# One normalization for two groups of heads, an output projection over full rows, and another rule for starting exponentials on VectorE

## The chip, the cores and the metric

The kernel runs on one core of one Trainium2 chip. Its time is the device time of one launch in microseconds (us), the median of several runs. The profile is of one further execution. Its span runs from the first to the last instruction that the profiler saw; the device time of the same execution lies a little above the span.

## The reference

One adaLN transformer block over 2048 tokens of width 512, in bf16:

```python
mod = silu(c) @ w_mod                       # six vectors sa, ca, ga, sb, cb, gb of 512
h = layernorm(x) * (1 + ca) + sa
q, k, v = h @ wqkv                          # 32 heads of 16
p = softmax(q @ k.T * 16 ** -0.5)           # per head 2048 x 2048
x = x + ga * ((p @ v) @ wo)
h = layernorm(x) * (1 + cb) + sb
x = x + gb * ((gelu(h @ w_gate) * (h @ w_up)) @ w_down)      # inner width 1792
```

The 32 score matrices have 134 million entries, and each needs an exponential. That is 2048 tiles of 128 keys by 512 columns of queries.

## The kernel before, in words

**Attention.** The heads are taken in eight groups of four, numbered qd from 0 to 7. Group qd uses the 128-row chunk qd // 2 of the transposed q and k. A chunk holds eight heads of 16 rows, that is four strips of 32 rows with an even and an odd head each. An even qd takes the even heads (k in `kme`, with the odd heads' rows set to zero) and an odd qd the odd heads (`kmo`). The tokens, as queries, are cut into six sets (`SETS`): three of 512, one of 256, two of 128. A *unit* is one group of heads with one set of queries. For the first QS groups the two sets of 128 are joined to one unit of 256. So the last units in order are: before, the joined groups 0 to 4, then set 4 with groups 5, 6, 7, then set 5 with groups 5, 6, 7.

A unit runs through its keys in *rounds*; a round is four score tiles (banks of PSUM, 128 x 512), one for each head. The score matmuls (`qk`) of up to four banks run in four row strips of TensorE. Each bank then needs an exponential, and there are two ways:

- ScalarE takes two or three banks in one ACTIVATE (`E<-ps_sc`, 128x1024 or 128x1536) and writes to E, a ring of NSL slots.
- VectorE takes a whole round, a *quad*. One instruction for each bank turns the score into the bits of a bf16 number (`dreg<-ps_sc`, `mreg<-ps_sc`, or `<-ps_mi` where the bank of side work is borrowed). Then three *shifts* over 128x2048 (`mreg<-dreg`, `mreg<-mreg`), on VectorE or GpSimd, add constants to these bits, and the four results go through four passes of the value matmul, in place of one. Only rounds whose key tiles lie from QA to QB can be quads.

The value matmuls (`pv_mms`, `ps_pv<-E,vaug`) have 17 output rows for each head: 16 sums, and in row 16 the sum of the exponentials. The four heads of a unit stand in rows 0, 32, 64, 96 of the accumulator.

**End of a unit** (`unit_end`). VectorE copies the accumulator to `osb`. On the queue of SyncE (SP), a chain of DMAs brings the four rows of sums to DRAM and back over 128 partitions (`scr_den<-osb`, `den<-scr_den`), VectorE takes reciprocals (`rden<-den`), and DMAs write them to DRAM and spread each over 32 rows (`scr_rec<-rden`, four times `rb<-scr_rec`). VectorE multiplies (`onorm<-osb,rb`). A unit's range of `osb` is in `self.live` until then, and the last value matmul of a later unit that needs this range is held back (`blocked`). Groups 6 and 7 of the two last sets avoid the DMAs: `near_end` spreads the sums with a small matmul.

**Output projection.** `onorm` has eight slots, one for each group. Of its 128 rows only 4 x 16 are of use. `wo` has its rows placed to match, and zeros elsewhere. For each tile of 128 tokens `wo_mm` runs eight matmuls of 128 rows by 512 columns, and `mm` cuts each into four of 32 output rows (not in the tail).

**Order.** All instructions are written out ahead of time by one program. It keeps its own estimate of when each engine is free, and at each step (`stream`) appends either the next score matmuls with their exponentials, a value matmul, a piece of side work (projections, output projection, FFN, all through the one bank `ps_mi`), or a filler matmul that keeps TensorE busy. The position `pos` counts score banks from 0 to 2048. Each piece of side work has a first position and a due position, and `credit` grows so that it gets done in time. A quad begins only if a buffer and a candidate round are there and, past `ends[2]` (position 1536), only if the credit is below CREDIT, so while there is little side work owing. Element-wise steps and DMAs are tasks that are appended to VectorE, ScalarE or SP when the estimate says that they can start.

On the chip each engine works through its list in order, and waits where a semaphore is not there yet. SP's queue carries the chains of the sums, the weights of the FFN (256 KB each, streamed for the first four sets, then kept for the two last sets) and the outputs.

**The tail** (`tail`) comes after the last exponential: the FFN of the last two tiles, and for the last tile also the output projection and the second layernorm.

Of the kernel before, what the change touches and what calls it, by code (L numbers as in the profile page):

```python
# [32 lines left out]
BCOL = (0, 0, 0, 0, 0, 128)  # L33
QS = 5
CH = 3
SC = 2 * CH
NSL = 18
assert NSL % CH == 0
# [3 lines left out]
NS = 4  # L42
AHEAD = 20
PREFER = 300
LAND = 1500
SIDE = 1024
PRESS = 5
HOT = 1
# [5 lines left out]
SLIP = 0  # L54
QA = 5
QB = 13
# [402 lines left out]
class _Kernel(_Recorder):  # L459
# [12 lines left out]
    def alloc(self):  # L472
# [33 lines left out]
        self.kq = [mreg[:, 12288:14336], dreg[:, 0:2048], dreg[:, 2048:4096]]  # L506
        self.wo = sb("wo", [P, 8, D], BF16)
        self.E = sb("E", [P, NSL, 512], BF16)
        self.onorm = sb("onorm", [P, 8, 512], BF16)
        self.ga = sb("ga", [P, D], BF16)  # L510
# [313 lines left out]
    def side_mod(self):  # L824
        mi = self.mi[:, :]
        if not self.dry:
            self.task([lambda dc=dc: self.ts("dve", self.scbc[:, dc, :], self.ones, self.sc_bf[:, dc:dc + 1],
                                             None, ALU.mult) for dc in range(NDC)], "scbc")
        yield from self.until("scbc")
        for dst, k, s in ((self.ga, 2, 1.0), (self.gb, 5, 0.5)):  # L830
            for dc in range(NDC):
                yield 512, lambda dc=dc, k=k: self.mm(mi, self.scbc[:, dc, :], self.mod_w(dc, 512 * k, 512),
                                                      start=(dc == 0), stop=(dc == NDC - 1))
            self.ts("dve", dst[:, :], mi, s, None, ALU.mult)
            yield END
        if not self.dry:
            self.task([lambda qd=qd: self.tt("dve", self.wo[:, qd, :], self.wo[:, qd, :], self.ga[:, :], ALU.mult)
                       for qd in range(8)], "wo")
        yield 512, lambda: self.mod_cols(mi[:, 0:8], 1536)
        self.copy("dve", self.modB[:, :], mi[:, 0:8])  # L840
        self.ts("dve", self.modB[:, 4:8], self.modB[:, 4:8], 1.0, None, ALU.add)
        self.done("modB")
        if not self.dry:
            self.sq_free.extend(range(NS))
        yield END

    def side_wo_load(self):

        if not self.dry:
            self.task([lambda qd=qd: self.memset("dve", self.wo[:, qd, :], 0.0) for qd in range(8)]  # L850
                      + [lambda: self.memset("dve", self.self32[:, :], 0.0)], "wo0")
        yield from self.until("wo0")
        selv = self.self32[:, :].rearrange("p (a b) -> p a b", b=32)
        self.affine_select(selv, [[-32, 4], [0, 32]], ALU.not_equal, 1.0, -16, 1)
        for j in range(4):
            for ee in range(2):
                src = self.A_wo.rearrange("(a j e r) n -> j e r a n", j=4, e=2, r=DH)[j, ee]
                self.dma("sp", self.wo[32 * j:32 * j + DH, ee:8:2, :], src, "wo%d" % (2 * j + ee))
        yield END
# [24 lines left out]

    def wo_mm(self, bank, gi, tl, qd, first=True):
        c = OCOL[gi] + P * tl
        self.mm(bank, self.onorm[:, qd, c:c + P], self.wo[:, qd, :], start=first and qd == 0, stop=(qd == 7))

# [14 lines left out]
    def near_end(self, k, qd, den):  # L903

        q0, W = SETS[k]
        yield from self.until(("osb", k, qd))
        _, lo, hi = self.osb_span(((k,), qd, q0, W))
        osb, rb = self.osb[:, lo:hi], self.rb[:, lo:hi]
        yield 4 * W, lambda: self.mm(den, self.self32[:, :], osb)

        def fin():
            self.tt("dve", self.onorm[:, qd, OCOL[k]:OCOL[k] + W], osb, rb, ALU.mult)
        if not self.dry:
            self.task([lambda: self.recip(rb, den)], ("rec", k, qd))
        yield from self.until(("rec", k, qd))
        if not self.dry:
            self.task([fin], ("onorm", k, qd))
        yield END

    def side_wo(self, gi):  # L920
# [4 lines left out]
        yield from self.until("wo")  # L925
        for qd in range(8):
            yield from self.until(("onorm", gi, qd))
        for i in range(n):
            for qd in range(8):
                yield 512, lambda i=i, qd=qd: self.wo_mm(mi, gi, i, qd)  # L930
            self.wo_fin(mi, tiles[i])
# [281 lines left out]
    def stream(self):  # L1213
# [133 lines left out]
        while cg <= group[units[-1]]:  # L1347
# [12 lines left out]
            if tq is not None and tq <= t + 30:  # L1360
# [6 lines left out]
                if short > FILL - FLOOR or slack > 213 and short > 0:  # L1367
                    self.mm(self.scp[:, s0, :], *filler)
                    continue
                g = None  # L1370
                if len(mem) == CH and pos >= FIRST and not self.pressed() and self.free["dve"] + 600 < max(self.free["act"], t + 480) + 880 + LATE:
                    while quad is None and cand and rounds[cand[0]][2] < pos + (AHEAD1 if rounds[cand[0]][2] < nsplit else AHEAD):
                        cand.pop(0)
                    if quad is not None:
                        g = quad["rnd"][2]
                    elif (cand and self.quad_free and (pos < ends[2] or self.credit < CREDIT) and rounds[cand[0]][2] < pos + 96 and self.backlog() < BACK
                          and all(k in self.have for k in self.keys(seq[rounds[cand[0]][2]]))):
# [8 lines left out]
                if g is not None:  # L1386
                    for n in (CH, CH - 1):
                        if n == CH and (self.open or self.credit > SIDE
                                        or self.probe(lambda: self.mm(self.mi[:, 0:P], *filler)) > t + 30):
# [140 lines left out]
    def unit_end(self, u, acc):  # L1530
# [5 lines left out]
        if sets[0] >= len(SETS) - 2 and len(sets) == 1 and qd >= 6:  # L1536
            self.done(("osb", sets[0], qd))
            return
        self.live[u] = (lo, hi)
        m = 4 * W // P  # L1540
        o = 8 if BCOL[sets[0]] else 0
# [5 lines left out]
        def rd(j):  # L1547
            self.dma("sp", self.rb[32 * j:32 * j + 32, lo:hi],
                     s2[W * j:W * j + W].rearrange("(o n) -> o n", o=1).broadcast_to([32, W]), "dd%d%d" % (sem, j))

        def fin2():
            c = OCOL[sets[0]]
            self.tt("dve", self.onorm[:, qd, c:c + W], osb, rb, ALU.mult)
            if self.probing is None:
                self.live.pop(u)
                for k in sets:
                    self.done(("onorm", k, qd))

        def free():
            c = OCOL[sets[0]]  # L1560
            return ("den", u) in self.have and all(
                ("wo", k) in self.have for k in range(sets[0]) if OCOL[k] < c + W and c < OCOL[k] + SETS[k][1])
# [3 lines left out]
                  + [("sp", lambda j=j: rd(j)) for j in range(4)], ("den", u))  # L1566
        self.task([fin2], None, free)

# [46 lines left out]
    def tail_end(self, k):  # L1615
# [7 lines left out]
        yield lambda: self.mm(bank, self.ident[:, :], self.xs[:, tile, :], start=True, stop=False)  # L1623
        for qd in range(8):
            yield from self.until(("onorm", k, qd))
            yield lambda qd=qd: self.wo_mm(bank, k, 0, qd, False)
        self.task([lambda: self.ln_stat(tile, bank)] + self.ln2_steps(k, bank), ("ln2", k))
# [94 lines left out]
```

## Time and profile before

| | before |
|---|---|
| median of 7 runs | 824.65 us (823.65 to 829.19) |
| profiled execution: time | 825.47 us |
| profiled execution: span | 823.6 us |
| busy: TensorE, VectorE, ScalarE, GpSimd | 765.7, 682.4, 788.2, 225.8 us |
| E<-ps_sc 128x1024 and 128x1536 on ScalarE | 416 and 273 |
| scores to bf16 bits on VectorE | 396 (99 quads) |
| granted TensorE clock, mean | 0.996 |

The busy time of an engine is the time in which it had at least one instruction under way. ScalarE's instructions overlap a little: one starts before the last has ended, so the mean duration in a row of the profile is longer than the distance from start to start.

### The profile page before, as it was taken

The numbers are of one execution on the slowest core, as the hardware profiler recorded it, in microseconds if no ns is written. First come the engines' busy times: TensorE is split into PE (matmuls) and PEld (weight loads), VectorE is DVE, ScalarE is ACT, GpSimd is POOL, SyncE is SP. The second block draws the span as 40 slices with busy tenths as digits, with TensorE's granted clock in tenths as the row PEclk, the third lists the DMA queues.
The fourth block names the chain that finished last, engine by engine and source line by source line (L and its number), as shares of the span: only waits on it lengthen the run. The fifth ranks groups of instructions, "written<-read, shape, count | busy, mean of one in ns | idle before, by whom it ended". The sixth has DMA issues, their size and how long they took to land.

```text
span 823.6 us, 27926 instructions
## 1 busy us (share of the span) xinstructions
PE 765.7 (93%) x12508; PEld 274.8 (33%) x12513; DVE 682.4 (83%) x1304; ACT 788.2 (96%) x745; POOL 225.8 (27%) x129
## 2 busy tenths in 40 slices
PE   8899999989899999899999998999998989978988
PEld 3334333322222222222222222222443423435556
DVE  7978998998888889899989988999577977756754
ACT  4999999999999999999999999999999999998982
POOL 1000331051654655562464375441000000000000
PEclk9999999999999999999999999999999999999999
DMA  9001000000002112111100221212122222077330
GB/s 313 21 7 35 19 16 16 17 16 16 15 14 69 48 37 64 28 54 54 35 16 23 72 87 31 58 47 66 37 68 84 62 76 58 23 219 220 82 80 14
DMA packets 74930, 47.66 MB, mean 58 GB/s; under 512 B 17693, under 2 KB 70618, under 8 KB 74810
## 3 DMA queue, kind: packets, MB, share of 16 engines
q1 hardware_dynamic: 72426, 44.30, 18.9%
q8 instruction: 98, 1.61, 0.8%
q10 hardware_dynamic: 2384, 1.57, 0.6%
q14 instruction: 22, 0.18, 0.1%
HBM read 43.25 MB, written 2.61 MB: 56 GB/s over the span
## 4 chain that ended last, share of the span: by engine, by line
ACT 87%; PE 8%; DMA 2%; DVE 2%; issue 0%; POOL 0%; SPq 0%; DVEq 0%; POOLq 0%
ACT E L366 84%; PE ps_sc L353 3%; PE ps_mi L353 3%; ACT wreg L366 2%; DMA mreg<-in_w_mod_dram 1%; PE ps_pv L353 1%; DMA mreg<-in_B_w_gate_dram 1%; DMA mreg<-in_B_w_up_dram 1%; DVE wreg L387 0%; DVE wreg L383 0%; POOL mreg L378 0%; PE ps_sc L357 0%; DVE wreg L370 0%; DVE kme L378 0%; DVE xs L370 0%
## 5 line engine op out<-in xcount | busy, mean ns | idle before, releaser
L366 ACT ACTIVATE E<-ps_sc 128x1024 bf16<-128x1024 f32 (+2 forms) x698 | 760.2, 1274 | 19.4 <-PE ps_sc L353 18.6
L378 DVE TENSOR_SCALAR dreg<-ps_sc 128x512 uint16<-128x512 f32 x260 | 176.7, 686 | 32.5 <-PE ps_sc L353 29.6
L353 PE MATMUL ps_sc<-qT,kme 32*128 32x512 bf16 (+2 forms) x1342 | 175.4, 332 | 17.4 <-ACT E L366 15.7
L378 POOL TENSOR_SCALAR mreg<-dreg 128x2048 uint16<-128x2048 uint16 x79 | 148.8, 1901 | 154.9 <-DVE mreg L378 37.5
L353 PE MATMUL ps_sc<-qT,kmo 32*128 32x512 bf16 (+2 forms) x1402 | 179.4, 323 | 12.8 <-ACT E L366 11.6
L353 PE MATMUL ps_pv<-E,vaug 128*17 128x512 bf16 (+2 forms) x2236 | 152.4, 321 | 2.1 <-DVE nwt L370 0.8
L353 PE MATMUL ps_mi<-wreg,mreg 128*32 128x512 bf16 (+1 forms) x1792 | 113.6, 358 | 10.6 <-DVE wreg L383 3.0
L353 PE MATMUL ps_pv<-mreg,vaug 128*17 128x512 bf16 (+2 forms) x1500 | 115.5, 349 | 1.0 <-DVE mreg L378 0.2
L378 POOL TENSOR_SCALAR mreg<-mreg 128x2048 uint16<-128x2048 uint16 x39 | 73.8, 1900 | 121.7 <-DVE mreg L378 71.2
L378 DVE TENSOR_SCALAR mreg<-ps_sc 128x512 uint16<-128x512 f32 x128 | 87.1, 687 | 18.3 <-PE ps_sc L353 17.0
L353 PEld LDWEIGHTS ps_sc<-qT,kme 32*128 32x128 bf16 x1342 | 46.5, 91 | 150.0 <-ACT E L366 125.7
L353 PEld LDWEIGHTS ps_sc<-qT,kmo 32*128 32x128 bf16 x1402 | 48.5, 91 | 128.6 <-ACT E L366 104.8
L378 DVE TENSOR_SCALAR mreg<-dreg 128x2048 uint16<-128x2048 uint16 x119 | 78.7, 685 | 2.9 <-PE ps_pv L353 2.7
L353 PEld LDWEIGHTS ps_pv<-E,vaug 128*17 128x17 bf16 x2236 | 45.0, 89 | 63.6 <-issue 52.3
L353 PEld LDWEIGHTS ps_mi<-wreg,mreg 128*32 128x32 bf16 x1792 | 39.0, 96 | 56.4 <-issue 15.3
L353 PEld LDWEIGHTS ps_pv<-mreg,vaug 128*17 128x17 bf16 x1500 | 33.8, 89 | 38.7 <-issue 17.7
L387 DVE CAST wreg<-ps_mi 128x512 bf16<-128x512 f32 x49 | 33.6, 685 | 11.1 <-PE ps_mi L353 10.9
L383 DVE SCALAR_TENSOR_TENSOR wreg<-wreg,ps_mi 128x512 bf16<-128x512 bf16 x49 | 33.5, 683 | 10.1 <-PE ps_mi L353 7.6
L378 DVE TENSOR_SCALAR mreg<-mreg 128x2048 uint16<-128x2048 uint16 x60 | 40.4, 683 | 1.6 <-PE ps_pv L353 1.4
L353 PE MATMUL ps_mi<-hreg,wreg 128*32 128x512 bf16 x480 | 38.0, 384 | 0.4 <-DVE mreg L378 0.2
L353 PE MATMUL ps_mi<-wo,onorm 128*32 128x512 bf16 x480 | 35.2, 381 | 0.0
L353 PE MATMUL ps_mi<-mreg,hreg 128*32 128x512 bf16 x448 | 35.0, 381 | 0.0
(146 smaller groups left out, 609.1 us busy)
## 6 DMA issues: line engine op xcount, KB each, us to landing
mreg<-in_B_w_up_dram SPq DMA_DIRECT2D x32, 256.0 KB, 3.3
mreg<-in_B_w_gate_dram SPq DMA_DIRECT2D x28, 256.0 KB, 3.0
rb<-scr_rec SPq DMA_DIRECT2D x96, 64.0 KB, 2.0
mreg<-in_B_w_down_dram SPq DMA_DIRECT2D x16, 256.0 KB, 2.7
dreg<-in_B_w_down_dram SPq DMA_DIRECT2D x12, 256.0 KB, 4.7
mreg<-in_w_mod_dram SPq DMA_DIRECT2D x1, 2048.0 KB, 14.3
out_dram<-xs SPq DMA_DIRECT2D x16, 128.0 KB, 1.7
rb<-scr_rec SPq DMA_DIRECT2D x52, 32.0 KB, 2.1
```

The source lines that it names most:

```text
L353: return self.rec("pe", lambda e: e.matmul(out, lhsT, rhs, start=start, stop=stop, tile_position=tp), [lhsT, rhs], [out], cost=(n, int(rhs ...
L366: return self.rec("act", lambda e: e.activation(out, in_, func, scale=scale, **kw), rd, wr, cost=self.cost("act", out, [in_], "act"))
L378: return self.rec(eng, lambda e: e.tensor_scalar(out, a, s1, s2, **kw), rd, [out], cost=self.cost(eng, out, [a], "ts"))
L383: return self.rec("dve", lambda e: e.scalar_tensor_tensor(out, a, s, b, op0=op0, op1=op1), rd, [out], cost=self.cost("dve", out, [a, b], " ...
L387: return self.rec(eng, lambda e: e.tensor_copy(out, in_), [in_], [out], cost=self.cost(eng, out, [in_], "ts"))
```

## The change

**Pairs of groups.** The end of an even unit leaves its sums in `osb` and spreads its reciprocals over 16 rows of each strip in place of 32. The end of the odd unit of the same pair spreads its own reciprocals over the other 16 rows of the same columns of `rb`, and four DMAs (`move`) bring its sums from rows 0 to 15 of each strip of its own columns of `osb` to rows 16 to 31 of the even unit's columns. One multiplication then makes all 128 rows of a slot of `onorm`, which now has four slots. The even unit's range of `osb` stays in `self.live` until that multiplication, the odd unit's until its last move is issued.

**Full rows.** The output projection has four matmuls for each tile and takes `wo` as it lies in DRAM. The two last sets have five: three pairs, and groups 6 and 7 by themselves, through `onormp` and two extra slots of `wo`.

**Units and quads.** QS is 6, so group 5 of the last two sets is a joined unit too. E has 24 slots in place of 18. Quads may use key tiles from 6 on (before: 5), and begin at least 24 positions ahead (before: 20). Past position 1536 a quad may also begin when there is no side work, or when the next piece is blocked for over 2000 ns by the program's own estimate (`idle`); in that case it may also borrow the bank of side work.

```diff
 SETS = ((0, 512), (512, 512), (1024, 512), (1536, 256), (1792, 128), (1920, 128))
-QS = 5
+QS = 6
-NSL = 18
+NSL = 24
-AHEAD = 20
+AHEAD = 24
+IDLE = 2000
-QA = 5
+QA = 6
 # alloc
-        self.wo = sb("wo", [P, 8, D], BF16)
+        self.wo = sb("wo", [P, NDC + 2, D], BF16)
-        self.onorm = sb("onorm", [P, 8, 512], BF16)
+        self.onorm = sb("onorm", [P, NDC, 512], BF16)
+        self.onormp = sb("onormp", [P, 2, 256], BF16)
 # side_wo_load (the memsets now cover slots 4 and 5, side_mod scales 6 slots)
+        for dc in range(NDC):
+            self.dma("sp", self.wo[:, dc, :], self.A_wo[P * dc:P * dc + P, :], "wo%d" % dc)
         for j in range(4):
-            for ee in range(2):
-                src = self.A_wo.rearrange("(a j e r) n -> j e r a n", j=4, e=2, r=DH)[j, ee]
-                self.dma("sp", self.wo[32 * j:32 * j + DH, ee:8:2, :], src, "wo%d" % (2 * j + ee))
+            src = self.A_wo.rearrange("(a j e r) n -> j a r e n", j=4, e=2, r=DH)[j, NDC - 1]
+            self.dma("sp", self.wo[32 * j:32 * j + DH, NDC:NDC + 2, :], src, "wo%d" % (NDC + j))
+    def wo_parts(self, gi):
+        return [0, 1, 2, 3] if gi < len(SETS) - 2 else [0, 1, 2, "n6", "n7"]
+
-    def wo_mm(self, bank, gi, tl, qd, first=True):
+    def wo_mm(self, bank, gi, tl, part, first=True):
         c = OCOL[gi] + P * tl
-        self.mm(bank, self.onorm[:, qd, c:c + P], self.wo[:, qd, :], start=first and qd == 0, stop=(qd == 7))
+        if isinstance(part, int):
+            lhs, rhs = self.onorm[:, part, c:c + P], self.wo[:, part, :]
+        else:
+            i = int(part[1]) - 6
+            lhs, rhs = self.onormp[:, i, BCOL[gi]:BCOL[gi] + P], self.wo[:, NDC + i, :]
+        self.mm(bank, lhs, rhs, start=first and part == 0, stop=part == self.wo_parts(gi)[-1])
 # near_end writes onormp[:, qd - 6, ...]; side_wo and tail_end loop over wo_parts
 # stream
+                idle = w is None or self.probe(w[4][1]) > t + IDLE
-                    elif (cand and self.quad_free and (pos < ends[2] or self.credit < CREDIT) and ...
+                    elif (cand and self.quad_free and (pos < ends[2] or self.credit < CREDIT or idle) and ...
-                        if n == CH and (self.open or self.credit > SIDE
+                        if n == CH and (self.open or (self.credit > SIDE and not idle)
 # unit_end
         self.live[u] = (lo, hi)
+        self.done(("osb", u))
+        odd = qd % 2
+        first = (sets, qd - odd, q0, W)
+        _, lo0, hi0 = self.osb_span(first)
         def rd(j):
-            self.dma("sp", self.rb[32 * j:32 * j + 32, lo:hi],
-                     s2[W * j:W * j + W].rearrange("(o n) -> o n", o=1).broadcast_to([32, W]), "dd%d%d" % (sem, j))
+            p = 32 * j + DH * odd
+            self.dma("sp", self.rb[p:p + DH, lo0:hi0],
+                     s2[W * j:W * j + W].rearrange("(o n) -> o n", o=1).broadcast_to([DH, W]), "dd%d%d" % (sem, j))
+
+        def move(j):
+            self.dma("sp", self.osb[32 * j + DH:32 * j + 32, lo0:hi0], self.osb[32 * j:32 * j + DH, lo:hi], "mv%d%d" % (sem, j))
+            if j == 3 and self.probing is None:
+                self.live.pop(u)
         def fin2():
-            self.tt("dve", self.onorm[:, qd, c:c + W], osb, rb, ALU.mult)
+            self.tt("dve", self.onorm[:, qd // 2, c:c + W], self.osb[:, lo0:hi0], self.rb[:, lo0:hi0], ALU.mult)
-        self.task([fin2], None, free)
+        if odd:
+            self.task([("sp", lambda j=j: move(j)) for j in range(4)], ("den", "move", u), self.after([("osb", first)]))
+            self.task([fin2], None, free)
```

## The prediction

> **What bounds the kernel now.** I read the page's busy times and the engines' shares of the chain that ended last first. In both ScalarE stands at the top.
>
> ```profile
> PE 765.7 (93%) x12508; PEld 274.8 (33%) x12513; DVE 682.4 (83%) x1304; ACT 788.2 (96%) x745; POOL 225.8 (27%) x129
> ...
> ACT 87%; PE 8%; DMA 2%; DVE 2%; issue 0%; POOL 0%; SPq 0%; DVEq 0%; POOLq 0%
> ```
>
> Such shares hide stages, so next came busy time by stretches of 20 us. The columns are TensorE, weight loads, VectorE, ScalarE, GpSimd, clock, DMA share and GB/s.
>
> ```profile
> 560.00:580.00 20.00, 18.71 (x284) 5.89 (x281) 17.19 (x30) 20.00 (x18) 0.00 (x0) 1.00 0.17 49
> 580.00:600.00 20.00, 19.75 (x401) 8.18 (x396) 8.46 (x18) 20.00 (x17) 0.00 (x0) 1.00 0.14 37
> ...
> 740.00:760.00 20.00, 16.45 (x434) 9.74 (x436) 12.74 (x28) 16.07 (x14) 0.00 (x0) 0.91 0.77 223
> ...
> 800.00:820.00 20.00, 19.49 (x250) 15.24 (x252) 9.49 (x25) 5.54 (x11) 0.00 (x0) 1.00 0.01 2
> ```
>
> From 20 to 740 us ScalarE has hardly a gap. VectorE, in contrast, idles 11.5 of 20 us at 580 to 600, and GpSimd does nothing past 560. From 740 on ScalarE has gaps, and after the last exponential (797.5) comes a tail on TensorE. The chain in order of time shows what makes the gaps: waits for weights.
>
> ```profile
> 736.14 5.63 DMA mreg<-in_B_w_gate_dram
> ...
> 759.33 4.83 DMA mreg<-in_B_w_up_dram
> ```
>
> So time is saved where ScalarE gets fewer exponentials, and hardly elsewhere. What is one worth? The timeline of ScalarE, from start to start (durations overlap):
>
> ```profile
> 560.83 1.50 ACT L366 ACTIVATE E<-ps_sc 128x1536 bf16<-128x1536 f32 x1
> 562.16 1.11 ACT L366 ACTIVATE wreg<-wreg 128x1024 bf16<-128x1024 bf16 x1
> 563.11 1.08 ACT L366 ACTIVATE E<-ps_sc 128x1024 bf16<-128x1024 f32 x1
> 564.01 1.11 ACT L366 ACTIVATE wreg<-wreg 128x1024 bf16<-128x1024 bf16 x1
> ```
>
> One of three banks takes 1.33 us here, one of two 0.90. Over all that follow each other without a gap the means are 1.337 and 0.920 us; I use these.
>
> **The quads, which pay.** The build order of the changed kernel holds 405 exponentials of two banks (416 before), 274 of three (273) and none of one bank (1 before): 1632 banks for 1652. The missing 20 are five more quads, 104 for 99. By the value matmuls, 86 lie in the three sets of 512 in both kernels, and 16 for 11 in units of 256 columns: the gain is past position 1536, where the profile shows VectorE free. ScalarE saves 11 x 0.920 + 0.50 (one bank, an estimate from the step of 0.42 us per bank) - 1.337 = **9.3 us**.
>
> Not all of that may count. Of the new quads about one net begins where FFN of set 3 runs (736 to 780 us before), and there the chain goes over TensorE. A quad is worth 1.85 us (9.3 / 5), so between 0 and 1.85 is lost; I take the middle, **+0.9**.
>
> **VectorE's bill.** These rows give the prices:
>
> ```profile
> L378 DVE TENSOR_SCALAR dreg<-ps_sc 128x512 uint16<-128x512 f32 x260 | 176.7, 686 | 32.5 <-PE ps_sc L353 29.6 <-POOL mreg L378 0.8
> ...
> L378 DVE TENSOR_SCALAR mreg<-dreg 128x2048 uint16<-128x2048 uint16 x119 | 78.7, 685 | 2.9 <-PE ps_pv L353 2.7
> ...
> L353 PE MATMUL ps_mi<-wo,onorm 128*32 128x512 bf16 x480 | 35.2, 381 | 0.0
> ...
> L370 DVE TENSOR_TENSOR onorm<-osb,rb 128x512 bf16<-128x512 f32 x24 | 16.4, 683 | 0.0
> ```
>
> Scores to bits: 20 more x 0.686 = +13.7 us. Shifts: 26 more on VectorE (205 for 179) x 0.684 = +17.8; 11 of them leave GpSimd (107 for 118). Multiplications to `onorm`: 12 x 0.683 + 6 x 0.418 + 2 x 0.288 less = -11.3. `wo`: two scalings and six memsets less, -2.4. The rest is -0.3. In all +17.5 us, 700 of some 814 us, 86% for 83%. The new quads' own 5 x (4 x 0.686 + 3 x 0.684) = 24 us go to 560 to 740, where VectorE idles some 46 us; that covers them. Without this cover each us late would be a us on ScalarE.
>
> **TensorE's bill.** The output projection loses 244 matmuls of 32 rows and gains 8 for the groups 6 and 7. Four run side by side; the tail's five matmuls in 1.24 us give 0.215 us per step, so 236 / 4 x 0.215 = -12.7 us. The quads' extra passes of value matmuls add about +3. ScalarE hides TensorE's gain: the weight loads of score matmuls wait for it 240.9 us in total. So the best-looking part of the change is worth nothing by itself.
>
> **Moves and chains on SP.** 76 moves are added (48 of 32 KB, 28 of 16 KB); SP issues 69 DMAs more in all, since the small units of group 5 fall away. The page "DMA: Bandwidth & Descriptors" of the Trainium skill (section "Anatomy of one DMA — SWDGE (gpsimd) path") gives a DMA a fixed cost of about 2 us, and its section on bandwidth advises large transfers and calls those under 64 KB dominated by descriptors. That speaks against this change: 76 x 2 = 152 us, an estimate by the rule, if each stood alone. The nearest row in the trace is the spreading of reciprocals, also on SP, four at a time:
>
> ```profile
> L417 SPq DMA_DIRECT2D rb<-scr_rec x156: 302/421/1721, 80.1 to 797.7; - x156
> ...
> DMA to landing us min/median/max: 1.7/2.1/4.4
> ```
>
> The rule's 2 us is there as time to landing, but four go out 0.42 us apart, so a pair's moves hold SP for 1.7 us (19 x 1.7 = 32 us in the whole run). They do not wait for reciprocals, so they land beside the chain of sums. SP itself waits for VectorE's `osb` alone 196.4 us in total, so I take 0 on the path; behind a move stand weights and reciprocals, and SP's 1.7 us delays these at most.
>
> What is late next is the buffer. An even unit's `osb` now stays until the pair is multiplied. For units of 512 that takes about one chain after the odd unit's end, and these end 20 to 25 us apart. A chain measured at the end of set 2 took from 577.6 to 591.9, 14.3 us; with moves 16. It fits. The tightest place is there: the first unit of set 3 needs the columns of the last pair of set 2, and in the changed order its copy stands directly behind that multiplication on VectorE. Between the two, 38 banks go to ScalarE at 0.45 us, 17 us. The margin is about 1 us, each us beyond costs one; range 0 to 4 (another 2.9 us for the slowest landings seen), I take 0.
>
> **Weights.** In the changed order of SP the third gate chunk of set 3, the one waited for at 736, has eight weight loads between it and the first four chunks; before, nine. Weights landed 0.7 us apart there, so **-0.7**; from 0 (the order of the wait only shifts) to -1.5.
>
> **Tail.** Three matmuls less, -0.6. But with QS at 6 set 4 now ends two units before the last, not three: its layernorm's transposes stand behind the last scores, where before two or three score groups followed. A transpose pair and its modulation (0.3 + 0.6 us) may lie bare, +0.6; range 0 to 2. Sum 0.
>
> **Sum.** Span 823.6 - 9.3 + 0.9 - 0.7 = 814.5. The profiled execution took 825.47, 1.87 above its span, so 816.4; it lay 0.82 above the median of the runs. 824.65 - 9.1 = **815.5 us** as a median.
>
> **The rivals.**
>
> *Part is given back* (chance 0.13). The buffer at the start of set 3 comes late, or set 4's chain at the end: the multiplication waits for `rb`, behind it on VectorE stand the next copies, and for these waits TensorE. For it: the margin of 1 us, and landings of up to 4.4 us. Against it: the larger ring E bridges six banks more (2.7 us). 815.5 + 2 to 6: about 819.
>
> *The quads' gain is idle* (0.06). If the end of the attention is set by FFN of set 3 with its weights and not by ScalarE, then 9.3 us of exponentials only make gaps. For it: the chain from 730 to 780. Against it: ScalarE's gaps in there are under 5 us, so it is nearly the bound itself. Then 824.
>
> *VectorE becomes the bound* (0.07, slower). From 100 to 560 us it is busy 17 to 19 of 20 us. The 11 shifts that leave GpSimd, and any that run late, hold back the value matmuls that wait for them, and then E's ring and ScalarE. It decides once over 12.6 us (9.1 + 2.5 + 1.0 for the margins) of VectorE's additional work lie bare. If all 17.5 do: 815.5 + 17.5 = 833. Against it: in that stretch the multiplications saved (8.2 us) pay for the shifts (7.5 us).
>
> *The idle rule begins nothing* can be left out: the five quads are in the build order.
>
> **How the numbers follow.** The likeliest case, 815.5, has 0.74 and its own range 811.5 to 818.5: below by 0.8 (weights), 0.9 (quads without loss), 0.6 (tail) and the loss of small gaps; above by 3 of the 4 us that the buffer can cost. A measurement of this kernel tells 0.3%, 2.5 us, from no change. Faster: 0.74 + 0.13 = 0.87; same 0.06; slower 0.07. The range from 811 to 821 leaves out the two last cases (0.13), the upper end of the first rival (0.03) and 0.03 below.
>
> **What would show it.** Right: 405 and 274 exponentials with unchanged distances, ScalarE's busy time near 779, no new gap of over 1 us in it before 740 us, VectorE at 86%, the wait for the gate chunk at 5 us or less, a tail of 26 us. Wrong: a gap on ScalarE at the first unit of set 3 (around 585 to 600 us), VectorE's copies of `osb` late behind a multiplication, shifts that wait on GpSimd, or a tail of 28 us and more.

## The result and the profile after

The changed kernel takes 819.74 us (median of 13 runs, 817.17 to 824.15) against 824.57 for the kernel before beside it: a ratio of 0.9935 (95% interval 0.992 to 0.9951), or 5.4 us. Forecast were 9.1 us less, 0.989. So the direction held, and some 4 us of the gain are missing. The time lies in the stated range of 811 to 821 us, but above the 811.5 to 818.5 of the likeliest case: the range held because it took in the first rival.

The busy times and the engines' shares of the chain that ended last, of the changed kernel:

```profile
PE 753.2 (92%) x12273; PEld 268.4 (33%) x12278; DVE 695.5 (85%) x1320; ACT 779.5 (95%) x734; POOL 205.0 (25%) x118
...
ACT 76%; PE 13%; DMA 5%; DVE 3%; SPq 1%; issue 1%; ACTq 0%; DVEq 0%
```

ScalarE has 779.5 us for 788.2, as forecast (near 779). But its share of the chain fell from 87 to 76%, while TensorE's grew from 8 to 13 and DMA's from 2 to 5: other work now ends last more often. The groups, each shape apart, say that the planned savings are all there:

```profile
L367 ACT ACTIVATE E<-ps_sc 128x1024 bf16<-128x1024 f32 x405 | 399.7, 1117 | 2.9 <-PE ps_sc L354 2.8
L367 ACT ACTIVATE E<-ps_sc 128x1536 bf16<-128x1536 f32 x274 | 395.1, 1529 | 8.7 <-PE ps_sc L354 8.0 <-PE ps_mi L354 0.3
...
L379 DVE TENSOR_SCALAR mreg<-dreg 128x2048 uint16<-128x2048 uint16 x129 | 84.6, 683 | 2.3 <-PE ps_pv L354 2.0
...
L354 PE MATMUL ps_mi<-wo,onorm 128*32 128x512 bf16 x236 | 18.1, 383 | 1.6 <-DVE onorm L371 1.3 <-DVE dreg L379 0.3
```

405 and 274 exponentials with unchanged durations; shifts as forecast; the output projection's matmuls of 32 rows are 236 + 8 for 480. The column that changed is the one behind the second bar: the idle time before the exponentials. Stretches of 20 us (TensorE, weight loads, VectorE, ScalarE, GpSimd, clock, DMA share, GB/s) tell where. First one stretch of the kernel before, then the changed kernel:

```profile
620.00:640.00 20.00, 17.52 (x307) 6.49 (x310) 15.92 (x32) 20.00 (x18) 0.00 (x0) 1.00 0.34 96
```

```profile
580.00:600.00 20.00, 18.68 (x370) 7.20 (x362) 16.09 (x28) 20.00 (x19) 3.44 (x2) 1.00 0.08 19
620.00:640.00 20.00, 17.74 (x312) 5.99 (x304) 13.28 (x24) 17.70 (x16) 0.00 (x0) 0.91 0.34 94
740.00:760.00 20.00, 18.11 (x494) 10.53 (x486) 15.18 (x33) 18.70 (x18) 0.00 (x0) 1.00 0.66 185
...
800.00:820.00 20.00, 14.88 (x187) 11.43 (x188) 8.14 (x19) 4.45 (x9) 0.00 (x0) 0.97 0.04 14
```

At 580 to 600, where the forecast was worried about the buffer, ScalarE is full. At 620 to 640 it lacks 2.3 us, where it had no gap before.

All of a span can be split at ScalarE: the time to the first exponential; the work from there to the last exponential; in it the gaps of over 0.15 us; and what comes after the last one.

| profiled execution | to the first | work | gaps | after the last | span |
|---|---|---|---|---|---|
| before | 16.7 | 775.5 | 5.3 | 26.1 | 823.6 |
| changed | 16.5 | 766.7 | 9.1 | 26.6 | 818.9 |

The work fell by 8.8 us (forecast 9.3). The gaps took 3.7 of it back, the end 0.5. These gaps are what there is to explain: 2.3 us more in 600 to 720, 0.45 more in the FFN of set 3 (720 to 770), and 0.95 at 788. (A profile shows one execution: this one took 820.61 us, 0.9 above its kernel's median.) The first one is followed back here: the timelines of ScalarE, TensorE, VectorE and SP, each with start, duration, instruction and, in brackets, the idle time before it and what ended it.

```profile
636.78 1.02 ACT L367 ACTIVATE E<-ps_sc 128x1024 bf16<-128x1024 f32 x1 [1.31 <-PE ps_sc L354]
638.79 4.20 ACT L367 ACTIVATE E<-ps_sc 128x1024 bf16<-128x1024 f32 x4 [0.99 <-PE ps_sc L354]
```

```profile
632.46 1.05 PE L354 MATMUL ps_mi<-wreg,mreg 128*32 128x512 bf16 x16 [1.51 <-DVE wreg L384]
...
634.30 1.90 PE L354 MATMUL ps_mi<-wreg,mreg 128*32 128x512 bf16 x16
```

```profile
631.32 0.20 DVE L391 RECIPROCAL rden<-den 128x8 f32<-128x8 f32 x1 [1.60 <-DMA den<-scr_den]
...
631.73 0.68 DVE L384 SCALAR_TENSOR_TENSOR wreg<-wreg,ps_mi 128x512 bf16<-128x512 bf16 x1
```

```profile
623.21 0.54 SPq L418 DMA_DIRECT2D scr_den<-osb  x1
623.79 2.46 SPq L418 DMA_DIRECT2D osb<-osb  x4
626.29 0.58 SPq L418 DMA_DIRECT2D mreg<-in_B_w_gate_dram  x1
626.92 0.50 SPq L418 DMA_DIRECT2D den<-scr_den  x1
```

Read upwards: SP issues the sums, then four moves (2.46 us), then a gate load, and only then `den`. VectorE stands 1.60 us at the reciprocal, because its instructions go in order; behind it stands the FFN's `wreg`, for which TensorE waits 1.51 us; its scores come late, and ScalarE idles. The chain of waits holds this place and two more:

```profile
626.92 4.38 DMA den<-scr_den
...
730.65 6.32 DMA mreg<-in_B_w_gate_dram
...
777.64 4.96 DMA scr_rec<-rden
783.92 3.03 DMA rb<-scr_rec
787.07 0.44 DVE onorm L371
```

The gate chunk of set 3 was in it before (5.63 us). The last three lines are new: the last pair's multiplication waits 1.25 us for `rb`, TensorE for it, and ScalarE idles 0.95 us at 788. And a move is dearer than forecast:

```profile
L418 SPq DMA_DIRECT2D osb<-osb x76: 513/589/1417, 74.7 to 771.9; - x76
...
DMA to landing us min/median/max: 1.7/1.9/4.0
```

It holds SP for 0.59 us (0.42 was taken), 76 of them 45 us; a pair's four take 2.46 us where 1.7 was forecast.

### The profile page after: what moved, and what is told of

It is laid out like the page before. It is cut to its first block, busy times and chain, and to the rows that moved or that the text cites. A ratio compares the mean times of both kernels' runs of the same rounds, so it can differ in the third digit from the quotient of the medians.

```text
span 818.9 us, 27542 instructions
## 1 busy us (share of the span) xinstructions
PE 753.2 (92%) x12273; PEld 268.4 (33%) x12278; DVE 695.5 (85%) x1320; ACT 779.5 (95%) x734; POOL 205.0 (25%) x118
## 4 chain that ended last, share of the span: by engine, by line
ACT 76%; PE 13%; DMA 5%; DVE 3%; SPq 1%; issue 1%; ACTq 0%; DVEq 0%
ACT E L367 74%; PE ps_mi L354 6%; PE ps_sc L354 5%; ACT wreg L367 2%; PE ps_pv L354 2%; DMA xs<-in_A_x_dram 2%; SPq L418 1%; DMA mreg<-in_B_w_gate_dram 1%; DMA scr_rec<-rden 1%; DMA mreg<-in_B_w_up_dram 1%; DMA den<-scr_den 1%; DVE wreg L371 0%; DVE wreg L384 0%; DVE dreg L379 0%; DMA rb<-scr_rec 0%
## 5 line engine op out<-in xcount | busy, mean ns | idle before, releaser
L367 ACT ACTIVATE E<-ps_sc 128x1024 bf16<-128x1024 f32 (+2 forms) x687 | 751.4, 1274 | 24.9 <-PE ps_sc L354 24.1
L379 DVE TENSOR_SCALAR dreg<-ps_sc 128x512 uint16<-128x512 f32 x247 | 167.9, 686 | 28.0 <-PE ps_sc L354 25.1
L354 PE MATMUL ps_sc<-qT,kme 32*128 32x512 bf16 (+2 forms) x1321 | 166.7, 332 | 15.5 <-ACT E L367 14.0
L354 PE MATMUL ps_sc<-qT,kmo 32*128 32x512 bf16 (+2 forms) x1315 | 166.9, 332 | 12.1 <-ACT E L367 11.1
L354 PE MATMUL ps_mi<-wreg,mreg 128*32 128x512 bf16 (+1 forms) x1792 | 118.9, 361 | 11.7 <-DVE wreg L384 4.0
L354 PE MATMUL ps_pv<-mreg,vaug 128*17 128x512 bf16 (+2 forms) x1644 | 120.1, 343 | 2.5 <-DVE mreg L379 1.2
L379 DVE TENSOR_SCALAR mreg<-dreg 128x2048 uint16<-128x2048 uint16 x129 | 84.6, 683 | 2.3 <-PE ps_pv L354 2.0
L379 POOL TENSOR_SCALAR mreg<-mreg 128x2048 uint16<-128x2048 uint16 x29 | 54.6, 1897 | 87.6 <-DVE mreg L379 66.2
L379 DVE TENSOR_SCALAR mreg<-mreg 128x2048 uint16<-128x2048 uint16 x76 | 50.9, 692 | 0.9 <-PE ps_pv L354 0.7
L371 DVE TENSOR_TENSOR wreg<-wreg 128x1024 bf16<-128x1024 bf16 (+1 forms) x56 | 34.4, 619 | 0.5
```

The source lines that it names most:

```text
L354: return self.rec("pe", lambda e: e.matmul(out, lhsT, rhs, start=start, stop=stop, tile_position=tp), [lhsT, rhs], [out], cost=(n, int(rhs ...
L367: return self.rec("act", lambda e: e.activation(out, in_, func, scale=scale, **kw), rd, wr, cost=self.cost("act", out, [in_], "act"))
L371: return self.rec(eng, lambda e: e.tensor_tensor(out, a, b, op), [a, b], [out], cost=self.cost(eng, out, [a, b], "tt"))
L379: return self.rec(eng, lambda e: e.tensor_scalar(out, a, s1, s2, **kw), rd, [out], cost=self.cost(eng, out, [a], "ts"))
```

## The experiments

**One part alone.** The pairing with the idle rule off:

```diff
-                idle = w is None or self.probe(w[4][1]) > t + IDLE
+                idle = False
```

> The pairing alone: the changed kernel with the idle rule off (idle = False). It holds 100 quads (before 99, changed 104), 11 of them begun past position 1536 (12 and 17), and 423 exponentials of two banks, 267 of three, one of one: at 0.92, 1.337 and 0.50 us that is 746.6 us, 1.6 less than before and 7.7 more than the changed kernel. Theory (the quads pay, the moves and the longer chains of sums on SP cost): 824.6 - 1.6 + 0 to 3 = 823 to 826, no faster than before by more than 0.2%. Rival (the pairing pays by itself, through the lighter TensorE and the fewer multiplications): 819 to 821, near the changed kernel.

Measured: 828.16 us, ratio 1.0043 (1.0024 to 1.0061). The pairing alone doesn't pay, as the theory had it; it even costs more than said. In its trace the gaps are 15.2 us for 5.3 before, but this was its slowest execution (833.42 us).

The idle rule in the kernel before:

```diff
+                idle = w is None or self.probe(w[4][1]) > t + IDLE
...
-pos < ends[2] or self.credit < CREDIT)
+pos < ends[2] or self.credit < CREDIT or idle)
...
-self.credit > SIDE
+(self.credit > SIDE and not idle)
```

> The idle rule alone: the kernel before with the idle rule added (IDLE 2000, in both places), no pairing, no moves, ring E of 18, QS 5. 103 quads, 16 begun past position 1536; 392 exponentials of two banks and 284 of three: 740.3 us, 7.9 less than before. Theory (exponentials are worth their full time, and what is given back comes with the moves): 824.6 - 7.9 + 0 to 1 = 817 to 818, that is faster than the changed kernel. Rival (quads begun past 1536 are worth about half wherever they come from, since FFN of set 3 with its weights and the tail set the end): 824.6 - 4 = 820 to 821.

Measured: 837.9 us, ratio 1.0153 (1.0132 to 1.0175). Both expectations missed, the theory's by 20 us. ScalarE's timeline shows why:

```profile
789.29 1.55 ACT L367 ACTIVATE E<-ps_sc 128x1536 bf16<-128x1536 f32 x1
...
814.00 0.60 ACT L367 ACTIVATE E<-ps_sc 128x512 bf16<-128x512 f32 x1 [21.65 <-PE ps_sc L354]
```

The exponentials did end early, at 790.8 us, but the FFN of set 3 was not done. Counted in the traces, 1953 of the 2048 score banks stand before its first gate matmul (1912 before the change, 1915 in the changed kernel; the positions of the plan, which the expectations name, are some 12 to 20 lower). By the plan 18 400 of its 43 520 columns are left after the last score; in the trace these are 32 of its 448 gate and up matmuls and all 112 down matmuls. TensorE works them off alone, with ScalarE idle. So past 1536 there are two bounds, and a quad moves the work from one to the other: it takes banks from ScalarE, and the scores go by faster than the FFN beside them.

A test of this: let the rule begin still more quads in the changed kernel.

```diff
-IDLE = 2000
+IDLE = 500
```

> The changed kernel with IDLE 500 for 2000: the rule begins quads already at a wait of 0.5 us. 109 quads, 22 past position 1536; 425 exponentials of two banks and 254 of three: 730.6 us, 8.3 less than the changed kernel. In the plan FFN of set 3 then begins its matmuls at position 1974 (changed kernel 1903), and has some 28 000 of its 43 520 columns left when the last score is out, where the run with the idle rule alone had 18 400 left and stood 21.6 us between its last two long exponentials and the tail. Theory (past position 1536 there are two bounds: ScalarE's exponentials and the FFN of set 3 on TensorE; a quad pays only as long as that FFN still ends before the last exponential): a hole of 25 to 35 us after the last long exponential, 835 to 842 us, slower than before. Rival (a quad is worth 1.85 us wherever it begins): 819.7 - 8 = 812.

Measured: 842.0 us, ratio 1.0198 (1.0173 to 1.0224), at the upper end of what the theory gave, 30 us from the rival. The work before the last exponential is the least of all kernels (756.5 us), and what comes after it 62.3 us:

```profile
819.40 0.60 ACT L367 ACTIVATE E<-ps_sc 128x512 bf16<-128x512 f32 x1 [25.00 <-PE ps_sc L354]
```

And fewer, where FFN surely ends in time:

```diff
+                idle = idle and ("ffn", 2) not in self.have
```

> The changed kernel, but the idle rule holds only until FFN of set 2 is done (then the old rule on the credit alone). 101 quads, 14 past position 1536; 396 exponentials of two banks and 284 of three: 744.0 us, 5.1 more than the changed kernel, 4.2 less than before. FFN of set 3 ends at position 1997 in the plan (changed 2004, before 1998). Theory (FFN ends in time in both, so exponentials count in full): 819.7 + 5.1 = 824 to 825.5, no gain left over before. Rival (the last three quads lie in FFN's stretch and are worth nothing there, so the gain comes from others): 820 to 821.

Measured: 826.64 us, ratio 1.0011 (0.9995 to 1.0026). With three quads less the whole gain is gone, as the theory said: by the ratios this is 6.3 us more than the changed kernel, where 5.1 were expected. The order is a fresh one here too (gaps of 11.5 us in an execution 2.6 us above the median), so part of the agreement can be luck.

**The moves, planned anew.** The moves behind the pair's chains:

```diff
             self.task([("sp", lambda j=j: move(j)) for j in range(4)], ("den", "move", u),
-                      self.after([("osb", first)]))
+                      self.after([("osb", first), ("den", u), ("den", first)]))
```

> The changed kernel, but the four moves of a pair are issued after both chains of sums (den, reciprocal, scr_rec, rb) instead of as soon as the odd sums stand in osb. 103 quads; 389 exponentials of two banks and 286 of three: 740.3 us, 1.4 more than the changed kernel. Theory (the moves ahead of den and rb in SP's order make reciprocals and multiplications late): the waits of VectorE for den and rb (about 6.5 us in five places and 1.25 at 787) and the gaps of ScalarE at 636 to 639 (2.3 us) go: 819.7 + 1.4 - 3 = 818. Against it: the multiplication now comes one set of moves (2 to 4 us) later and osb stays longer, which can cost 1 to 2. Rival (the order on SP doesn't matter): 821.

Measured: 837.94 us, ratio 1.0154 (1.0131 to 1.0177). This says nothing of the order on SP: FFN of set 3 was unfinished again at the last score, and 40.1 us come after the last exponential.

No moves at all:

```diff
-            self.dma("sp", self.osb[32 * j + DH:32 * j + 32, lo0:hi0], self.osb[32 * j:32 * j + DH, lo:hi], "mv%d%d" % (sem, j))
```

> The changed kernel without the 76 moves: the odd heads' sums are not brought beside the even heads' (that part of the computation is left out; all the rest stays). 105 quads; 410 exponentials of two banks, 269 of three and one of one: 737.4 us, 1.5 less than the changed kernel. Theory (SP's time for the moves gives back about 3 us): 819.7 - 1.5 - 3 = 815 to 816, with SP's chains den and scr_rec landing as before the change (VectorE waits for den under 1 us each). Rival (moves are free, as forecast, and the loss has another cause): 818.

Measured: 821.26 us, ratio 0.9957 (0.9944 to 0.997), not faster than the changed kernel. Inconclusive too: the work fell to 764.4 us and the gaps to 8.6, but 30.1 us come after the last exponential for 26.6. The last down matmuls of set 3 now stand behind 2041 score banks, counted in the traces, instead of 2008. The lesson of both: in this kernel every edit to a cost or a condition gives another order, and the order can be worth some 18 us (837.9 against 819.7, with 103 quads for 104). From here on the order was held.

**The moves, with the order held.** The kernel is planned as the changed one; then the finished list of instructions is edited and its dependences are worked out again. In the traces VectorE, ScalarE and GpSimd's element-wise work then have exactly the changed kernel's sequence.

```diff
+        ops = [o for o in ops if not o.stream.startswith("d_mv")]
```

> The order of every instruction on every engine as in the changed kernel, only the 76 moves left out of SP's queue (the odd heads' sums are not brought beside the even heads': that part of the computation is left out). Unlike the run without moves before, nothing is planned anew, so the time is the price of the moves alone. Theory A (the moves hold SP: the den transfer of the pair at 623 to 627 us and the later chains go out up to 2.4 us earlier): the gap of ScalarE at 636 to 639 (2.3 us) shrinks by at least half: 819.7 - 1 to - 2.5 = 817 to 818.5. Theory B (moves cost nothing on the path, as forecast; what made the chains late are weight loads of 256 KB ahead of den and scr_rec): within 0.7 of the changed kernel, 819 to 820.4.

Measured: 816.92 us, ratio 0.9889 (0.9868 to 0.9909). Theory A holds, and the time is even a little below its range: by the ratios the moves cost 0.9935 - 0.9889 = 0.46%, 3.8 us (1.6 to 5.9 by the two intervals). By the medians alone it is 2.8, as the kernel before took 825.64 beside this run and 824.57 beside the changed kernel. An execution's time also goes with its granted clock: the changed kernel's reach from 817.17 us at 0.997 to 824.15 at 0.990. At 0.997 it takes 817.2 to 818.0 us and this run 815.0. So the price is some 2 to 4 us. ScalarE and SP at the same place:

```profile
631.69 1.14 ACT L368 ACTIVATE wreg<-wreg 128x1024 bf16<-128x1024 bf16 x1
632.64 7.89 ACT L368 ACTIVATE E<-ps_sc 128x1536 bf16<-128x1536 f32 x7
```

```profile
621.91 0.50 SPq L419 DMA_DIRECT2D scr_den<-osb  x1
622.86 0.39 SPq L419 DMA_DIRECT2D mreg<-in_B_w_gate_dram  x1
623.52 0.34 SPq L419 DMA_DIRECT2D den<-scr_den  x1
```

`den` goes out 1.6 us after the sums, not 3.7, with the gate load still ahead of it, and ScalarE has no gap. (The first column differs from the changed kernel's by the 1.0 us by which this execution's first exponential came earlier.) Gaps in all: 4.4 us for 9.1, in an execution 2.5 us below this kernel's median; a table below has them by place.

The other suspect, weight loads ahead of the chains:

```diff
+        hoist(den, load)
+        for k in reversed(range(6)):
+            after(at("d_wu%d" % k, -1), at("d_dd13", -1))
```

> The order of every other engine as in the changed kernel; on SP alone two edits: den of the pair of set 3 that goes out at 626.9 us stands before the gate load instead of behind it, and the last pair's scr_rec and its four rb stand before the six B_w_up loads of the tail instead of behind three and six of them. Moves stay. If the weight loads ahead of the chains cause the two gaps: the gap at 636 to 639 (2.3 us) and the one at 788 (0.95, and about 0.5 of set 4's layernorm in the tail) go: 819.7 - 2 to - 3.7 = 816 to 817.7. If the moves cause them (theory A of the run without moves in the same order), or the gap at 636 comes from the slow group of FFN matmuls there, the first stays: 818.5 to 819.7.

Measured: 820.76 us, ratio 0.9944 (0.9923 to 0.9965): no gain, and above both ranges. The first edit caught the wrong pair, the next one (its `den` near 660 us); the `den` in question stayed behind its gate load, so that question is answered by the run before, not by this one. The second edit worked where it was made: VectorE no longer waits for the last `rb`, and the gap there fell from 0.95 to 0.60 us. But 3.2 us of gaps stood at 760 to 765, behind an up load that was waited for 4.96 us. The total didn't move.

Is it the moves' bytes or SP's time? The same 28 moves past position 1536, from GpSimd's queue:

```diff
+        for o in ops:
+            if o.stream[:4] in ("d_mv",) and int(o.tag[3][0].ap[-1][1]) == 256:
+                o.eng = "pool"
```

> The order of every instruction as in the changed kernel, but the 28 moves past position 1536 (units of 256 columns) go out from GpSimd's DMA queue, which has nothing else to do there, instead of SP's; the 48 before stay on SP. All 76 are done. If SP's time is what the moves cost (each holds SP for 0.59 us, and behind them stand den, scr_rec, rb and the FFN's weights): as without moves, 816 to 817.5. If it is their bytes and packets on the DMA engines, behind which weights and sums land later: 819 to 820.5, as the changed kernel. If they land much later from that queue, so that the multiplications come late: over 821.

Measured: 816.54 us, ratio 0.9895 (0.988 to 0.991), the time without moves, with all work done. It is SP's time, and that of these 28 moves: the 48 of the first sets still stand on SP and cost nothing that shows. On SP, and for the moves on GpSimd:

```profile
623.50 0.50 SPq L419 DMA_DIRECT2D scr_den<-osb  x1
624.45 0.39 SPq L419 DMA_DIRECT2D mreg<-in_B_w_gate_dram  x1
625.11 0.34 SPq L419 DMA_DIRECT2D den<-scr_den  x1
```

```profile
L419 POOL DMA_DIRECT2D osb<-osb x28: 484/484/992, 603.8 to 766.8; - x28
...
DMA to landing us min/median/max: 1.6/2.1/4.4
```

The moves land no sooner than from SP, but nothing stands behind them. The Trainium skill says of this, in "DMA: Bandwidth & Descriptors" (section "Issuing engines are not separate DMA queues"), that issuing from several engines saves only the sequencer's time to initiate a DMA, usually small beside the DMA itself. Per DMA the issue is the smaller part here too, though not by much: 0.59 against 1.9 us on SP, 0.48 against 2.1 on GpSimd. But of the moves' price it is SP's issue time that counts: the landing stayed, and the price went.

Where did ScalarE's gaps go? All over 0.15 us behind 600 us, in us, one execution each:

| | 600 to 720 | FFN of set 3 (720 to 770) | last pair (780 to 790) |
|---|---|---|---|
| before | 0 | 4.6 | 0 |
| changed | 2.3 | 5.0 | 0.95 |
| without moves | 0 | 3.2 | 0.56 |
| chains before weights | 1.1 | 5.9 | 0.60 |
| 28 moves on GpSimd | 0 | 3.3 | 1.21 |

So the moves' price has two halves: the late `den` at 636, and some 1.8 us in the FFN of set 3, where SP issues the weights between the chains. The gap at the last pair is hardly theirs: it stays without them and grows with the moves on GpSimd. There `scr_rec` and `rb` stand behind up loads, and only the run that took them ahead of these loads ended VectorE's wait (1.25 us; 1.51 with the moves on GpSimd).

With the 56 spreadings of reciprocals past 1536 on GpSimd as well:

```diff
-            if o.stream[:4] in ("d_mv",) and int(o.tag[3][0].ap[-1][1]) == 256:
+            if o.stream[:4] in ("d_mv", "d_dd") and int(o.tag[3][0].ap[-1][1]) == 256:
```

> The order of the changed kernel, with the 28 moves and also the 56 spreadings of reciprocals (rb<-scr_rec) past position 1536 on GpSimd's DMA queue. SP keeps the sums (scr_den, den, scr_rec) and the weights. With the moves alone there it took 816.5 (ratio 0.9895). If SP's time still holds weights and sums back in the FFN of set 3 (gap of 3.1 us at 736 and 1.2 at 785 in that run), 0.5 to 2 us more fall: 814.5 to 816. If these gaps are the weights' own landing, the same within 0.7: 816 to 817. If the spreadings are slower from that queue, the last multiplication comes later: 818.

Measured: 814.77 us, ratio 0.989 (0.9866 to 0.9914). By the ratios that is the same as with the moves alone; the gaps went from 5.3 to 4.8 us. Both beat the changed kernel.

The dose the other way, each move twice:

```diff
+        ops = [p for o in ops for p in ((o, o) if o.stream.startswith("d_mv") else (o,))]
```

> The order of the changed kernel with each of the 76 moves issued twice, one behind the other on SP (152 moves, same data). If the price is SP's time, it is paid again: the run without moves lies 0.46% (3.8 us) under the changed kernel, so this one 3 to 5 us over it: 823 to 825, with the gaps of ScalarE at 636 to 639 and in the FFN of set 3 (735 to 765) larger. The second of two equal moves waits for the first one's landing (about 2 us), which can add as much again. If only the late den at 636 mattered, 821.

Measured: 969.65 us, ratio 1.1761 (1.174 to 1.1781), 150 us over the changed kernel where 3 to 5 were expected. The second move waits on SP for the first one's landing, 113.3 us in 76 waits, and issuing 76 more takes about 0.5 us each: together about 152 us. That all of it comes through is what I hadn't expected, and VectorE's waits tell how:

```profile
ACT E L368 <- PE ps_sc L355: 151.6, 71, 9.9
...
DVE rden L392 <- DMA den<-scr_den: 133.8, 22, 9.3
```

The reciprocals have fixed places in VectorE's order. Eight more us on SP per pair, and VectorE stands at them, in the first sets too, where the single moves cost nothing. The slack there is a few us at most.

**Pairing alone, without its moves,** in its own held order (the filter on `d_mv` as above):

> The order of the run with pairing alone (idle rule off), without its 76 moves (the odd heads' sums are not brought over: left out). That run had 1.6 us less of exponentials than the kernel before and still came out at a ratio of 1.0043, some 5 us above what its exponentials say. If the moves on SP cost this, the ratio falls by about 0.5%: 0.998, 823 us. If it is the planning of the order without the idle rule: 1.002 to 1.004, 827 to 828.

Measured: 821.17 us, ratio 0.996 (0.9947 to 0.9972). The moves had cost 0.83% there, 6.8 us, where 0.5% was expected. Without them the pairing gains 3.3 us, more than its 1.6 us of exponentials.

## Why the prediction was right and where it was wrong

- *The quads* (-9.3): right. 405, 274 and no exponential of one bank; ScalarE's work fell by 8.8 us. With the moves out of SP's way the changed order gives 0.9889 to 0.9895, the forecast's 0.989. The small terms below missed by 0.5 to 0.9 us in both directions, and part of this agreement is that they cancel.
- *One quad in the FFN's stretch* (+0.9): gaps in 720 to 770 grew by 0.45, but that is the moves' doing; without them they are 3.2 us for 4.6 before. No loss of the quads is left to see.
- *VectorE* (+17.5, hidden): 13.1 more (4.4 under the sum, not followed further), 85%, and hidden: the run with GpSimd's moves does the same VectorE work in the same order and keeps the gain. The third rival falls.
- *TensorE* (-12.7 + 3, "worth nothing by itself"): its busy time fell 12.5. The pairing without moves gained some 1.7 us beyond its exponentials, so "nothing" was too little, or the multiplications saved on VectorE count, or that order was a lucky one; the runs don't tell these apart. Nor was any of QS, NSL, AHEAD and QA changed by itself.
- *Moves and chains on SP* ("I take 0 on the path"): **the step that failed.** It measured 3.8 us by the ratios (3.3 by the run on GpSimd), 2 to 3 at equal granted clock: most of what was missing. The step saw the weights and reciprocals behind a move and then dismissed them, since SP waits 196 us for `osb` in the whole run. That is an average. Behind a pair's moves, with one gate load between, stands the pair's own `den`, and VectorE has its reciprocal at a fixed place; behind the moves at 737 stand the weights that the FFN waits for. That they "land beside the chain of sums" was true of landing, not of issue, and SP's time for a pair was sized at 1.7 us, not 2.46. The Trainium skill's rule of 2 us (the section is on DMAs from GpSimd; here a move landed 1.9 us after its issue on SP and 2.1 on GpSimd) was right as a warning and wrong as a price: neither 152 us nor 0.
- *The buffer* (0, range 0 to 4): right. The last pair of set 2 waited 0.2 us for `rb`, with no gap at 580 to 600. The multiplication that came late was the last pair's, at 787, which the first rival had named as set 4's chain.
- *Weights* (-0.7): did not come. ScalarE's gap at the gate chunk was 3.1 us and is 3.2, and the wait in the chain grew to 6.3, where 5 or less was to be seen (5.7 without moves).
- *Tail* (0): +0.5.
- *The rivals.* The first (chance 0.13, about 819) has the time, and half of the mechanism: chains late on SP and work queued behind them on VectorE, but at a reciprocal and in the FFN of set 3, not at the buffer. The second (the gain is idle, 824) isn't what happened here, yet it was priced wrongly: where FFN of set 3 is late, the gain isn't just idle, it turns into 13 to 16 us of loss (837.9 and 842.0). That the changed kernel escapes this, FFN ending at position 2004 of 2048, I had not examined. What lets it in there, the lighter TensorE or the chance of the order, stays open: pairing with more quads misses it too, and so does the fresh order with 103 quads. That the forecast's direction held owes something to luck here.

## What to carry to other kernels

Price a small DMA twice: by its landing, and by the time that it holds the queue that issues it, and for the latter name what stands directly behind it and who waits for that at a fixed place. Here another engine's queue was free, and with it the second price was gone. And where a planner makes the order, test a cost with the order held; a fresh plan can cost more than what is tested.

## What the hardware showed that was not expected

A short wait on TensorE can cost twice. In the changed kernel the wait of 1.51 us at 632 was followed by a drop of the granted clock, and the next group of 16 matmuls took 1.90 instead of 1.05 us. In the run with the chains before the weights the same wait of 1.51 us left the clock alone, and the gaps of ScalarE were 1.07 us for 2.30. So about half of that gap is the clock's.

The traces hold the times of the granted clock, and these show what differs. In all 14 traces the clock falls to one half, for 3.41 us or two to four times as long (unless the end cuts it short), and within one execution every fall begins on one grid with a step of 3.41 us. Here are three steps of that grid in the changed kernel, then in that run (columns as above; the clock is the third from the end):

```profile
627.49:630.90 3.41, 2.94 (x58) 1.00 (x54) 1.66 (x3) 3.41 (x4) 0.00 (x0) 1.00 0.57 157
630.90:634.31 3.41, 1.76 (x36) 0.57 (x33) 2.41 (x6) 3.41 (x4) 0.00 (x0) 1.00 0.03 4
634.31:637.73 3.42, 3.42 (x38) 1.08 (x42) 1.95 (x3) 2.11 (x2) 0.00 (x0) 0.50 0.36 98
```

```profile
627.65:631.06 3.41, 2.29 (x48) 0.67 (x36) 1.67 (x4) 3.41 (x4) 0.00 (x0) 1.00 0.54 150
631.06:634.47 3.41, 2.41 (x46) 0.89 (x46) 2.78 (x5) 3.41 (x4) 0.00 (x0) 1.00 0.07 15
634.47:637.89 3.42, 3.27 (x66) 1.12 (x62) 2.48 (x4) 2.35 (x3) 0.00 (x0) 1.00 0.32 93
```

In the changed kernel the whole wait falls into one step, TensorE is busy for 1.76 of 3.41 us (52%), and the next step has half the clock. In the other run the wait lies across a border, both steps keep 67% and more, and nothing happens. The 14 traces together, by TensorE's busy share in a step at full clock: under 51% the clock fell in the next step in 50 of 50 cases, from 51 to 68% in 13 of 61, above that in none of 3185. (Busy time is in part modelled, which may blur the border.) So the share of busy time in a step decides, and where the grid happens to lie decides what one wait costs. That this makes the spread between executions of one kernel is likely, but not shown.

"TensorE: Matmul & The Clock Gate" of the Trainium skill (section "What's actually happening") halves the clock after an idle window of about 3.4 us. The length of the window agrees with the 3.41 us here. But the window need not be idle: half of it was enough, with 1.51 us as the longest wait.
